# A routed expert layer: the first rows are fetched by an index of their own, without their records

## The chip, the cores and the metric

The kernel runs on one core of one Trainium2 chip. The metric is the device time of one execution in microseconds, from the program's start to its end. "The trace" is what the hardware profiler recorded of one such execution.

## The reference

Two blocks follow one another on 2048 rows of 512 numbers, all in float32. The first is a convolution layer (H3), the second a mixture of eight experts of which each row takes exactly one:

```
h  = x + q_layer(layernorm(x), k, v)          # short convolution, product, long convolution, gate
xf = layernorm(h)                             # 2048 x 512
logits = xf @ w_gate                          # 2048 x 8
topk_idx = argsort(-logits)[:, :1]
gates = softmax(topk_val)                     # over one value
for e in range(8):
    w   = (gates * (topk_idx == e)).sum(-1, keepdims=True)
    out = out + w * (silu(xf @ w1[e]) @ w2[e])   # w1[e]: 512 x 1792, w2[e]: 1792 x 512
result = h + out
```

Only the second block, its beginning above all, is touched by the change.

## The kernel before

**Stage 1.** The convolution layer is run in an order that a planner sets (`plan.run`, line 598); it writes the rows of h to a DRAM buffer, h_dram. The change leaves that order alone. What stage 1 leaves to the second block is h, the routing logits in `lacc`, and for each row a record `rec` of four numbers: mean, reciprocal standard deviation, gate weight and a helper for it. In before, a row of h_dram is 516 wide: 512 numbers of h and the four of the record behind them, so whoever fetches a row has its record too.

**Routing** (lines 601 to 727). All rows lie on 128 partitions with 16 rows each. VectorE finds the largest logit (`mx`, `eq`, `cand`, `oh`), a scan and three small products on TensorE count the rows of each expert (`pn`) and number them within it (`pr`). The experts are ordered by their number of rows: `key`, then `gt` and `sr` (rank of each expert), `perm_i` (which expert stands at which rank). Each row gets a place, `c_i` = its rank's place times 4096 and its number; split into a tile `col_i` and a position in the tile `lo_f`. To turn the map round (from places to rows), line 679 marks the tile of each row (`ohhi`, 24 tiles), lines 685 to 687 mark the position in 16 steps (`ohlo`, one instruction and one product for each of the 16 rows of a partition), and the products add up to `ptab`: the row at each place. From it come `idxg` (indices for fetching, line 694) and `idxs` and `half_i` (for storing). `keep_warm` puts products on TensorE whose result nobody reads.

**The start of the experts.** GpSimd fetches the first expert's rows by `idxg` (line 707) into two tiles, `first0` and `first1`; SyncE reads the first expert's number from `perm_i` and starts the loads of its first two weight pieces (line 715). A flag `wide_i` chooses between branches for row counts of different sizes; with these inputs the experts are given 240, 304, 280, 264, 256, 248, 240 and 240 rows in that order, in tiles of at most 128 rows.

**The experts** (`experts`, lines 730 to 943). Each expert has 14 steps, seven for w1 ("up") and seven for w2 ("down"), each with a weight piece of 128 x 1024 float32. All products are made of three products of parts: weights and rows are split into a high and a low part. A step's weights are loaded by SyncE (`raw`, eight steps ahead), split four steps ahead by ScalarE (`whi`) and VectorE (`wlo`). Up makes two blocks of 128 columns with 12 products each (line 821); ScalarE takes Silu (`s`, three buffers), VectorE the high part (`hh`) and GpSimd the low part (`hl`, line 826). Down (lines 842 and 845) reads hh and hl. While one expert runs, the next one's rows are fetched (`gather`, line 759: one tile each in the last steps of up), normalised on VectorE with the row's mean and reciprocal deviation (`norm`, line 772), transposed on TensorE in the fourth, fifth and sixth step of down (`turn_x`, line 781) and split again (lines 782, 783). Finished rows are scaled and added to h on VectorE (`o`, line 856) and scattered to the output by an indirect DMA that GpSimd issues (line 857). The last expert's last tile is done in two halves at the very end (`store_by_halves`).

**Order.** Each engine takes its instructions in the order in which the program issues them; an indirect DMA stands in GpSimd's queue between its other instructions. At the end all engines pass a common block (shown at line 1119), in which GpSimd and SyncE drain their queues.

## Time and profile before

| what | value |
|---|---|
| median of three timed runs | 544.11 us (543.62 to 544.54) |
| the profiled execution | 544.39 us |
| its span, first to last instruction | 542.5 us |
| mean granted TensorE clock, as a share of 2.4 GHz | 0.991 |
| TensorE busy, share of the span | 519.1 us, 96% |
| VectorE, ScalarE, GpSimd busy | 405.6, 265.1 and 260.7 us |
| memory read, written | 95.96 MB, 8.47 MB |

The profiled execution's time is 1.9 us longer than its span; this lies outside the recorded instructions. Busy shares are averages over stages with different limits, so the stretches and the order in time below are of more use than the shares. In the rows, PE is TensorE's product, PEld its weight load, DVE VectorE, ACT ScalarE, POOL GpSimd and SP SyncE; a letter q behind an engine's name marks what its sequencer does. "L686" is line 686 of the kernel.

### The profile page before, as it was taken

What the parts mean: (1) busy time and instruction counts of PE and PEld (TensorE: products, weight loads), DVE (VectorE), ACT (ScalarE), POOL (GpSimd) and SP (SyncE); (2) the same over time, 40 slices, a digit from 0 to 9 for tenths busy, and PEclk for the clock granted to TensorE, in tenths of its full rate; (3) what the DMA queues carried; (4) which work ended last, traced back from release to release, by engine and by line L of the source; (5) the groups of instructions that cost most, each with busy time, mean ns of one, the idle gap of its engine ahead of it and who ended that gap; (6) DMA issues with size and microseconds to landing.
All of it is one profiled execution on the core that took longest, in us unless ns stands there. A gap on an engine that the chain in (4) does not pass through costs nothing. (4 is left out here: it accounts for less than half of the span.)

```text
span 542.5 us, 12152 instructions
## 1 busy us (share of the span) xinstructions
PE 519.1 (96%) x4812; PEld 451.9 (83%) x4812; DVE 405.6 (75%) x558; ACT 265.1 (49%) x410; POOL 260.7 (48%) x297
## 2 busy tenths in 40 slices
PE   9999989999998699999999999999999999999994
PEld 9867767767656469789999999999988988988973
DVE  3779899898997968859855784974884784785851
ACT  2697887544320346545435445545543644554520
POOL 0555659865641136618503921840760760851832
PEclk9999999999999989999999999999999999999998
DMA  8918786659661278674654665674676566576401
GB/s 285 380 55 261 236 276 195 179 153 287 187 170 43 60 263 320 218 256 166 199 182 140 204 199 166 189 259 141 206 219 233 180 210 231 194 219 205 155 2 41
DMA packets 42468, 105.26 MB, mean 194 GB/s; under 512 B 6480, under 2 KB 14800, under 8 KB 42018
## 3 DMA queue, kind: packets, MB, share of 16 engines
q1 hardware_dynamic: 39602, 95.89, 54.9%
q0 software_dynamic: 2800, 8.51, 4.9%
q8 instruction: 40, 0.66, 0.5%
q14 instruction: 26, 0.21, 0.1%
HBM read 95.96 MB, written 8.47 MB: 193 GB/s over the span
## 5 line engine op out<-in xcount | busy, mean ns | idle before, releaser
L826 POOL TENSOR_TENSOR hl<-s,hh 128x240 fp32r<-128x240 f32 (+5 forms) x112 | 114.4, 1035 | 162.2 <-DVE hh L825 161.7
L807 DVE TENSOR_TENSOR wlo<-raw,whi 128x1024 fp32r<-128x1024 f32 x112 | 160.5, 1443 | 38.8 <-ACT whi L806 35.2
L806 ACT ACTIVATE whi<-raw 128x1024 fp32r<-128x1024 f32 x112 | 114.6, 1051 | 3.5 <-DMA raw<-in_w_dram 3.5
L824 ACT ACTIVATE s<-acc 128x240 f32<-128x240 f32 (+5 forms) x112 | 43.1, 387 | 98.1 <-PE acc L821 63.4
L825 DVE CAST hh<-s 128x240 fp32r<-128x240 f32 (+5 forms) x112 | 55.0, 501 | 30.1 <-ACT s L824 29.9
L821 PE MATMUL acc<-xh,whi 128*128 128x240 f32 (+5 forms) x448 | 73.0, 285 | 0.1
L821 PE MATMUL acc<-xh,wlo 128*128 128x240 f32 (+5 forms) x448 | 72.0, 283 | 0.0
L821 PE MATMUL acc<-xl,whi 128*128 128x240 f32 (+5 forms) x448 | 71.9, 283 | 0.0
L821 PEld LDWEIGHTS acc<-xh,whi 128*128 128x128 f32 x448 | 61.7, 189 | 0.8 <-ACT xh L782 0.3
L821 PEld LDWEIGHTS acc<-xl,whi 128*128 128x128 f32 x448 | 61.6, 189 | 0.0
L821 PEld LDWEIGHTS acc<-xh,wlo 128*128 128x128 f32 x448 | 61.4, 189 | 0.0
L842 PE MATMUL acc<-whi,hh 128*128 128x512 f32 (+2 forms) x136 | 54.3, 399 | 0.0
L842 PE MATMUL acc<-whi,hl 128*128 128x512 f32 (+2 forms) x136 | 53.6, 394 | 0.0
L842 PE MATMUL acc<-wlo,hh 128*128 128x512 f32 (+2 forms) x136 | 53.5, 394 | 0.0
L265 POOL TENSOR_TENSOR acc<-acc,ac 128x512 f32<-128x512 f32 x26 | 33.1, 1280 | 37.1 <-ACT acc L253 19.2
L845 PE MATMUL acc<-hh,whi 128*128 128x304 f32 (+2 forms) x168 | 49.8, 296 | 0.0
L845 PE MATMUL acc<-hl,whi 128*128 128x304 f32 (+2 forms) x168 | 49.2, 293 | 0.0
L845 PE MATMUL acc<-hh,wlo 128*128 128x304 f32 (+2 forms) x168 | 49.1, 292 | 0.0
L296 ACT ACTIVATE st<-pa 128x512 f32<-128x512 f32 x64 | 37.3, 595 | 20.6 <-PE pa L293 20.3
L293 PEld LDWEIGHTS pa<-kv,tw 128*128 128x128 f32 x256 | 30.2, 191 | 12.2 <-ACT st L296 8.7
L293 PE MATMUL pa<-kv,tw 128*128 128x128 f32 x256 | 33.5, 282 | 2.2 <-ACT st L296 2.2
L782 ACT ACTIVATE xh<-pt 128x512 fp32r<-128x512 f32 (+5 forms) x18 | 9.6, 535 | 53.1 <-PE pt L781 53.1
(171 smaller groups left out, 878.2 us busy)
## 6 DMA issues: line engine op xcount, KB each, us to landing
raw<-in_w_dram SPq DMA_DIRECT2D x112, 512.0 KB
tv<-in_tab_v_dram SPq DMA_DIRECT2D x12, 512.0 KB
h<-in_q_dram SPq DMA_DIRECT2D x16, 256.0 KB
kt<-in_kt_dram SPq DMA_DIRECT2D x3, 1216.0 KB
v<-in_v_dram SPq DMA_DIRECT2D x12, 256.0 KB
kern<-in_ssm_dram SPq DMA_DIRECT2D x12, 256.0 KB
h<-in_x_dram SPq DMA_DIRECT2D x12, 256.0 KB
h_dram<-h SPq DMA_DIRECT2D x12, 256.0 KB
```

What stands on the lines that cost most here:

```text
L265: nc.gpsimd.tensor_add(T[a, c, u], T[a, c, u], T[b, c, u])
L293: nc.tensor.matmul(p[:, :, j], tw[:, u * UJ + j, r, :], src[:, j, :], start=True, stop=True)
L296: nc.scalar.activation(T["s" + kind, c][:, r * NU + u], T["pa", kind, c, u, r], AF.Copy)
L782: nc.scalar.activation(xh[:, at, r0:r0 + m], pt[:, :, :m], AF.Copy)
L806: nc.scalar.activation(whi, raw, AF.Copy)
L807: nc.vector.tensor_sub(wlo, raw, whi.bitcast(F32))
L821: nc.tensor.matmul(pu, a[:, k, fs], b[:, k, :], start=i == 0, stop=i == 3 * ND - 1)
L824: nc.scalar.activation(s, pu, AF.Silu)
L825: nc.vector.tensor_copy(hh[:, f, :], s)
L826: nc.gpsimd.tensor_sub(hl[:, f, :], s, hh[:, f, :].bitcast(F32))
L842: nc.tensor.matmul(pd[:ds_.stop - ds_.start], b[:, f, ds_], a[:, f % 2, :], start=f == 0 and i == 0, stop=f == last - 1 and i == 2)
L845: nc.tensor.matmul(pd, a[:, f % 2, ds_], b[:, f, :], start=f == 0 and i == 0, stop=f == 2 * NCH - 1 and i == 2)
```

## The change

The first expert's rows get a table of their own. Instead of ranking all experts first, VectorE takes the smallest key (`least`), whose last bits are that expert's number, and only two tiles (`tile0`) are marked for it (`there0`, `m0`). The places no longer hold the rank: they are the expert's number times 4096, given by one more product into `pr`, and the row's number. The 16 one-hot instructions become two, on 16-bit integers with both operands as tensors, over nine and seven of the 16 rows. A product with `m0` gives `ptab0`, from which `idx0` fetches the rows. All 24 tiles (`m24`), the ranks, `eqm_p` and `perm_i` follow behind it, and `other_tables` later sorts the table into the order of the experts.

Rows and records have buffers of their own in DRAM: a row of h_dram is 512 wide, `rec_dram` holds the four numbers of each row. Mean and reciprocal deviation of the first expert's rows are not fetched: they are split into three bf16 parts, marked (`v0`) and selected by 16 products with the one-hot matrix (`pv0`, `mr0`). For all other experts each tile is fetched by two indirect DMAs, first the rows' ones, then the records'.

Further: up makes its two blocks side by side (all products with the first pair of parts, then the second, then the third); `wlo` of the first weight piece is made in two halves; the three last scatters stand behind the branches instead of within them, from three tiles of their own (`ends`); the warm-up products are placed differently.

On VectorE in the routing, behind the places `c_i`; ohhi and ohlo_f are the marks of tile and position, pt is the table in PSUM. Before:

```order
L674 TENSOR_REDUCE c_i<-r_2402 128x16
L675 TENSOR_SCALAR col_i<-c_i 128x16
L676 SCALAR_TENSOR_TENSOR lo_f<-col_i,c_i 128x16
L679 TENSOR_TENSOR ohhi<-tile_b,col_i 128x384
L686 TENSOR_SCALAR ohlo_f<-iota_b,lo_f 128x128 x16
L691 TENSOR_TENSOR over<-key,rungs 1x128
L693 TENSOR_REDUCE nover<-over 1x16
L694 TENSOR_SCALAR idxg<-pt 128x24
```

The same place after the change, up to the marks of all tiles; kt is a buffer of tables that also holds iota, tile and the first rows:

```order
L684 TENSOR_REDUCE c_i<-r_2420 128x16
L685 TENSOR_SCALAR col_i<-c_i 128x16
L686 TENSOR_SCALAR lo_i<-c_i 128x16
L692 TENSOR_TENSOR kt<-kt,col_i 128x32
L693 TENSOR_TENSOR m_2425<-kt,tok_b 128x32
L705 TENSOR_TENSOR ohlo_f<-kt,lo_i 128x128x9
L705 TENSOR_TENSOR ohlo_f<-kt,lo_i 128x128x7
L714 TENSOR_SCALAR idx_78<-pt 128x2
L715 RECIPROCAL rec<-rec 128x16
L716 TENSOR_TENSOR rec<-rec 128x16
L719 TENSOR_TENSOR over<-key,rungs 1x128
```

The index for the first rows stands ahead of a reciprocal and the flags, and is made from two marks instead of sixteen. On GpSimd in the first expert, from the middle of up to the second expert's first hl (hr are the rows of the next expert; two hl are one step). Before:

```order
L826 TENSOR_TENSOR hl<-s,hh 128x240 x8
L1119 ISA
L759 DMA hr_12846<-h_dram,idxg 128x516
L826 TENSOR_TENSOR hl<-s,hh 128x240 x2
L1119 ISA
L759 DMA hr_12888<-h_dram,idxg 128x516
L826 TENSOR_TENSOR hl<-s,hh 128x240 x2
L1119 ISA
L759 DMA hr_12930<-h_dram,idxg 48x516
L826 TENSOR_TENSOR hl<-s,hh 128x240 x2
L826 TENSOR_TENSOR hl<-s,hh 128x304 x3
```

After the change, from the third gather of rows on (what stands ahead of it is as before, with rows of 512):

```order
L823 DMA hr_13112<-h_dram,idxg 48x512
L895 TENSOR_TENSOR hl<-s,hh 128x240 x2
L1205 ISA
L823 DMA rec_13163<-rec_dram,idxg 128x4
L1205 ISA
L823 DMA rec_13179<-rec_dram,idxg 128x4
L1205 ISA
L823 DMA rec_13203<-rec_dram,idxg 48x4
L1205 ISA
L823 DMA rec_13245<-rec_dram,idxg 128x4
L1205 ISA
L823 DMA rec_13272<-rec_dram,idxg 112x4
L895 TENSOR_TENSOR hl<-s,hh 128x304 x3
```

Five fetches of records have come behind the first expert's last hl: three for the second expert's tiles, and two for the first expert's own, whose gate weights are needed when its rows are stored.

The diff, cut to what the text speaks of:

```diff
-    h_dram = dram.tile([S, RW], F32, name="h_dram")
+    h_dram = dram.tile([S, D], F32, name="h_dram")
+    rec_dram = dram.tile([S, 4], F32, name="rec_dram")
...
+    iota_b = place_h[:, :P * NJ].rearrange("p (m j) -> p m j", j=NJ)
+    tile_b = place_h[:, P * NJ:(P + 24) * NJ].rearrange("p (c j) -> p c j", j=NJ)
...
+    nc.gpsimd.tensor_scalar(base_b, const("e").unsqueeze(2).to_broadcast([P, E, NJ]), 32.0, None, op0=ALU.mult)
+    nc.gpsimd.tensor_copy(tile_b, const("tile").unsqueeze(2).to_broadcast([P, 24, NJ]))
+    nc.gpsimd.tensor_copy(iota_b, const("iota").unsqueeze(2).to_broadcast([P, P, NJ]))
...
-    keep_warm(5, 128)
+    pr = ps_t.tile([P, E, NJ], F32, name="pr", bufs=1)
+    nc.tensor.matmul(pr, one_b, base_b, start=True, stop=False)
+    keep_warm(8, 128)
...
+    rest = eq[:, 0:2]
+    both = rec[:, :, 0:2].rearrange("p j i -> p i j")
+    nc.gpsimd.tensor_copy(parts[:, 0], both)
+    nc.gpsimd.tensor_sub(rest, both, parts[:, 0])
...
-    nc.gpsimd.tensor_mul(rec[:, :, 2], rec[:, :, 2], rec[:, :, 3])
-    nc.sync.dma_start(h_rows[:, :, D:RW], rec)
...
+    least = small([1], "least", I32)
+    with nc.allow_low_precision(reason="whole numbers under 32768"):
+        nc.vector.tensor_reduce(least, key, axis=AX.X, op=ALU.min)
+    nc.vector.tensor_scalar(least, least, E - 1, None, op0=ALU.bitwise_and)
+    for t in range(2):
+        nc.gpsimd.tensor_scalar(tile0[:, t], least.to_broadcast([P, NJ]), 32.0, float(t), op0=ALU.mult, op1=ALU.add)
...
+    r2 = small([E, NJ], "r2")
+    nc.vector.tensor_tensor(r2, pr, oh, op=ALU.mult)
+    with nc.allow_low_precision(reason="whole numbers under 32768"):
+        nc.vector.tensor_reduce(c_i, by_j(r2), axis=AX.X, op=ALU.add)
+    nc.vector.tensor_scalar(col_i, c_i, 7, None, op0=ALU.logical_shift_right)
+    nc.vector.tensor_scalar(lo_i, c_i, P - 1, None, op0=ALU.bitwise_and)
+
+    def marks(name, tiles_b, n):
+        there = m = small([n, NJ], name, F16)
...
+        nc.vector.tensor_tensor(there, tiles_b, col_i.unsqueeze(1).to_broadcast([P, n, NJ]), op=ALU.is_equal)
+        nc.vector.tensor_tensor(m, there, tok_b.unsqueeze(1).to_broadcast([P, n, NJ]), op=ALU.mult)
+        return there, m
+
+    there0, m0 = marks("m0", tile0, 2)
...
+    for i in range(3):
+        for w in range(2):
+            nc.gpsimd.tensor_tensor(v0[:, i, w], there0, parts[:, i, w].unsqueeze(1).to_broadcast([P, 2, NJ]), op=ALU.mult)
+    ohlo = ohlo_f.bitcast(F16).rearrange("p (m j) -> p m j", j=NJ)
+    ptab0 = ps_t.tile([P, 2], F32, name="pt")
+    for js in (range(0, 9), range(9, NJ)):
+        at = slice(js[0], js[-1] + 1)
+        nc.vector.tensor_tensor(ohlo[:, :, at], iota_b[:, :, at],
+                                lo_i[:, at].unsqueeze(1).to_broadcast([P, P, len(js)]), op=ALU.is_equal)
+        for j in js:
+            nc.tensor.matmul(ptab0, ohlo[:, :, j], m0[:, :, j], start=j == 0, stop=j == NJ - 1)
+    pv0 = ps_t.tile([P, 12], F32, name="pt")
+    for j in range(NJ):
+        nc.tensor.matmul(pv0, ohlo_f.bitcast(BF16).rearrange("p (m j) -> p m j", j=NJ)[:, :, j],
+                         v0[:, :, :, :, j].rearrange("p i w t -> p (i w t)"), start=j == 0, stop=j == NJ - 1)
+    keep_warm(1, 512)
+    nc.vector.tensor_scalar(idx0, ptab0, -1.0, 0.0, op0=ALU.add, op1=ALU.max)
+    nc.vector.reciprocal(rec[:, :, 2], rec[:, :, 3])
+    nc.vector.tensor_mul(rec[:, :, 2], rec[:, :, 2], rec[:, :, 3])
...
+    m24 = marks("m24", tile_b, 24)[1]
+    mr0 = small([2, 2], "mr0")
+    nc.vector.tensor_reduce(mr0, pv0.rearrange("p (i w t) -> p t w i", i=3, w=2), axis=AX.X, op=ALU.add)
+    nc.vector.tensor_scalar(mr0, mr0, 128.0, None, op0=ALU.mult)
+    ptab = ps_t.tile([P, 24], F32, name="pt")
+    for j in range(NJ):
+        nc.tensor.matmul(ptab, ohlo[:, :, j], m24[:, :, j], start=j == 0, stop=j == NJ - 1)
+    keep_warm(3, 384)
...
-    ohhi = small([NJ, 24], "ohhi", F16)
-    nc.vector.tensor_tensor(ohhi, tile_b.unsqueeze(1).to_broadcast([P, NJ, 24]), bc(col_i, 24),
-                            op=ALU.is_equal)
-    vt = small([NJ, 24], "vt", F16)
-    nc.gpsimd.tensor_tensor(vt, ohhi, bc(tok_b, 24), op=ALU.mult)
-    ohlo = ohlo_f.bitcast(F16).rearrange("p (j m) -> p j m", j=NJ)
-    ptab = ps_t.tile([P, 24], F32, name="pt")
-    for j in range(NJ):
-        nc.vector.tensor_scalar(ohlo[:, j, :], iota_b, lo_f[:, j:j + 1], None, op0=ALU.is_equal)
-        nc.tensor.matmul(ptab, ohlo[:, j, :], vt[:, j], start=j == 0, stop=j == NJ - 1)
-    keep_warm(4, 432)
...
-        hr = first.tile([P, RW], F32, name=f"first{t}")
-        col = 3 * ORDER[0] + t
         nc.gpsimd.indirect_dma_start(
-            out=hr, out_offset=None, in_=h_dram[:, :],
-            in_offset=bass.IndirectOffsetOnAxis(ap=idxg[:, col:col + 1], axis=0))
-        rows0.append(hr)
-    place0 = nc.sync.value_load(perm_i[0:1, ORDER[0]:ORDER[0] + 1], min_val=0, max_val=E - 1)
+            out=rows0[t], out_offset=None, in_=h_dram[:, :],
+            in_offset=bass.IndirectOffsetOnAxis(ap=idx0[:, t:t + 1], axis=0))
+    place0 = nc.sync.value_load(least[0:1], min_val=0, max_val=E - 1)
     raw0 = []
     for ch in range(2):
         raw = first.tile([P, 1024], F32, name=f"raw{ch}")
         nc.sync.dma_start(raw, w1[bass.ds(place0, 1), ch].rearrange("o p f -> (o p) f"))
         raw0.append(raw)
-
+    nc.sync.dma_start(rec_dram.rearrange("(p j) d -> p j d", j=NJ), rec)
...
+    def other_tables():
+        nc.vector.tensor_tensor(sel, eqm_p.unsqueeze(2).to_broadcast([P, E, 3, E]),
+                                tabs_e.rearrange("p e t -> p t e").unsqueeze(1).to_broadcast([P, E, 3, E]), op=ALU.mult)
+        nc.vector.tensor_reduce(tabs, sel.rearrange("p i t e -> p (i t) e"), axis=AX.X, op=ALU.add)
+        nc.vector.tensor_scalar(idxg, tabs, -1.0, 0.0, op0=ALU.add, op1=ALU.max)
...
+        def gather(n, i):
+            ts = tiles(n)
+            if i >= 2 * len(ts):
+                return
+            kind, src, width = ("hr", h_dram, D) if i < len(ts) else ("rec", rec_dram, 4)
+            t, r0, m, col = ts[i % len(ts)]
+            into = X[kind, n, t] = xp.tile([P, width], F32, name=f"{kind}{t}")
+            nc.gpsimd.indirect_dma_start(
+                out=into[:m, :], out_offset=None, in_=src[:, :],
+                in_offset=bass.IndirectOffsetOnAxis(ap=idxg[:m, col:col + 1], axis=0))
...
+            pus = [ps_u.tile([P, cap], F32, name="acc") for _ in fs]
+            for i, (a, b) in enumerate(((whi, xh), (wlo, xh), (whi, xl))):
+                for f, pu in zip(fs, pus):
+                    at = slice((f % 2) * P, (f % 2) * P + P)
+                    for k in range(ND):
+                        nc.tensor.matmul(pu, a[:, k, at], b[:, k, :], start=i == k == 0, stop=i == 2 and k == ND - 1)
+            for f, pu in zip(fs, pus):
+                s = xp.tile([P, cap], F32, name="s", bufs=3)
+                nc.scalar.activation(s, pu, AF.Silu)
+                nc.vector.tensor_copy(hh[:, f, :], s)
+                nc.gpsimd.tensor_sub(hl[:, f, :], s, hh[:, f, :].bitcast(F32))
...
+        def send(n, t, m, y, rows, at, o=None):
+            late = o is not None
+            o = (o if late else xp.tile([P, D], F32, name="o", bufs=3))[:m]
+            nc.vector.scalar_tensor_tensor(o, y, X["rec", n, t][:m, 2:3], rows, op0=ALU.mult, op1=ALU.add)
+            if not late:
+                scatter(out, at, o, S)
...
-        gather(0)
+                send(n, t, m, pd[:m], X["part"][:m, cols], None, ends[half + 1])
+
+        firsts, last = tiles(0)[:-1], tiles(0)[-1]
         for s in range(len(raw0)):
             load_w(s)
-        split(0)
-        norm(0, *tiles(0)[0])
+            split_hi(s)
+        norm(0, *firsts[0])
+        split_lo(0, 0, 512)
         for s in range(len(raw0), AHEAD):
             load_w(s, s < 6)
-        for a in tiles(0)[1:-1]:
+        for a in firsts[1:]:
             norm(0, *a)
         for half in range(2):
-            norm(0, *tiles(0)[-1], half)
-        for a in tiles(0)[:-1]:
+            norm(0, *last, half)
+        split_lo(0, 512, 1024)
+        for a in firsts:
             turn_x(0, *a)
+        warm = ps_u.tile([P, P], F32, name="acc")
+        for _ in range(3):
+            nc.tensor.matmul(warm, const("one"), cs[:, :P], start=True, stop=True)
         for half in range(2):
-            turn_x(0, *tiles(0)[-1], half)
-        for s in range(1, LEAD):
+            turn_x(0, *last, half)
+        split_lo(1)
+        other_tables()
+        for s in range(2, LEAD):
...
+                if r < 2 and n + 1 < E:
+                    gather(n + 1, r + 4)
+                if n == 0 and 3 <= r < 3 + len(tiles(0)):
+                    gather(0, r - 3 + len(tiles(0)))
                 if 3 <= r < 3 + len(nx):
                     turn_x(n + 1, *nx[r - 3])
...
+    scatter(out, idxs[:, end - 1:end], ends[0], S)
+    for i in range(2):
+        scatter(halves, half_i[:, i:i + 1], ends[i + 1], 2 * S)
```

## Rows read from the trace of the kernel before

**Rows 1.** The table of stretches: start and end in us, length, then busy us and number of instructions of PE, PEld, DVE, ACT and POOL, the granted TensorE clock (share of full), the DMA engines' busy share, GB/s. The first row is the routing, the next four are pieces of it, then the experts, then the tail.

```profile
182.30:198.56 16.26, 11.82 (x56) 7.47 (x56) 12.38 (x54) 5.65 (x11) 6.62 (x14) 0.79 0.44 117
184.45:187.87 3.42, 1.67 (x13) 1.42 (x12) 3.13 (x14) 2.19 (x5) 0.51 (x2) 1.00 0.22 8
187.87:191.28 3.41, 2.25 (x15) 1.54 (x15) 3.41 (x18) 0.00 (x0) 0.83 (x1) 0.50 0.27 29
191.28:194.70 3.42, 3.42 (x7) 1.83 (x8) 0.88 (x7) 1.25 (x2) 2.16 (x2) 0.50 0.86 310
194.70:198.56 3.86, 2.84 (x12) 1.26 (x11) 3.02 (x10) 1.00 (x3) 2.44 (x6) 1.00 0.64 186
198.56:534.80 336.24, 336.24 (x2384) 315.18 (x2384) 239.58 (x280) 161.39 (x253) 156.54 (x148) 1.00 0.59 195
534.80:542.50 7.70, 0.00 (x0) 0.00 (x0) 0.48 (x1) 0.00 (x0) 1.45 (x2) 0.80 0.18 58
```

**Rows 2.** The timeline of VectorE: a two-source f32 instruction from the end of stage 1, then the routing. Columns: start in us, duration in us, engine, line, operation, out and in with their shapes, number of instructions in the row (its duration is that of all of them), and in brackets idle time before it and what ended that.

```profile
172.35 0.69 DVE L372 TENSOR_TENSOR st<-st 128x512 f32<-128x512 f32 x1
...
183.48 0.26 DVE L627 RECIPROCAL rec<-rec 128x16 f32<-128x16 f32 x1
...
185.33 0.17 DVE L652 SCALAR_TENSOR_TENSOR key<-pn,cs 128x8 f32<-128x8 f32 x1
185.53 0.23 DVE L657 TENSOR_TENSOR gt<-key 128x64 f32<-128x64 f32 x1
...
186.19 0.27 DVE L668 SCALAR_TENSOR_TENSOR r<-sr,pt 128x128 f32<-128x128 f32 x1
186.49 0.29 DVE L670 TENSOR_TENSOR r<-r,oh 128x128 f32<-128x128 f32 x1
186.70 0.20 DVE L672 TENSOR_REDUCE perm_i<-eqe 1x8 int32<-1x64 f32 x1
186.83 0.35 DVE L674 TENSOR_REDUCE c_i<-r 128x16 int32<-128x128 f32 x1
...
187.52 0.55 DVE L679 TENSOR_TENSOR ohhi<-tile_b,col_i 128x384 f16<-128x384 bf16 x1
187.99 3.32 DVE L686 TENSOR_SCALAR ohlo_f<-iota_b,lo_f 128x128 f16<-128x128 f16 x16
...
191.73 0.16 DVE L694 TENSOR_SCALAR idxg<-pt 128x24 int32<-128x24 f32 x1
```

**Rows 3.** The timeline from the index to the first product of the first expert, all engines, columns as in rows 2; between them two weight loads of warm-up products (PEld), and below the summary of line 707's DMAs (time from issue to landing).

```profile
192.20 1.20 POOL L707 DMA_INDIRECT first<-h_dram,idxg  x1 [3.22 <-DVE wide_i L697]
192.99 0.34 PEld L607 LDWEIGHTS warm<-cs 128*128 128x128 f32 x1 [0.38 <-issue]
193.71 0.34 PEld L607 LDWEIGHTS warm<-cs 128*128 128x128 f32 x1 [0.38 <-issue]
194.67 1.22 DVE L807 TENSOR_TENSOR wlo<-raw,whi 128x1024 fp32r<-128x1024 f32 x1 [2.47 <-ACT whi L806]
195.82 0.55 DVE L772 TENSOR_SCALAR xr<-first 128x512 f32<-128x512 f32 x1
196.31 0.09 DVE L797 MEMSET raw<- 128x1 f32 x4
197.24 0.74 DVE L772 TENSOR_SCALAR xr<-first 112x256 f32<-112x256 f32 x2 [0.84 <-DMA first<-h_dram,idxg]
198.56 0.71 PE L821 MATMUL acc<-xh,whi 128*128 128x240 f32 x3
...
DMA to landing us min/median/max: 3.5/3.5/3.5
```

**Rows 4.** The timeline of the first expert's hl chain on GpSimd and of the handover to the second expert, columns as in rows 2; below the summary of the 17 gathers of line 759.

```profile
206.60 3.89 POOL L826 TENSOR_TENSOR hl<-s,hh 128x240 fp32r<-128x240 f32 x4 [9.19 <-DVE hh L825]
...
214.42 2.35 POOL L826 TENSOR_TENSOR hl<-s,hh 128x240 fp32r<-128x240 f32 x2 [0.23 <-DVE hh L825]
...
223.21 0.90 POOL L759 DMA_INDIRECT hr<-h_dram,idxg  x1 [0.16 <-issue]
224.12 1.39 POOL L826 TENSOR_TENSOR hl<-s,hh 128x240 fp32r<-128x240 f32 x2
226.53 0.54 DVE L772 TENSOR_SCALAR xr<-hr 128x512 f32<-128x512 f32 x1
227.35 0.60 PE L781 MATMUL pt<-cs,xr 128*128 128x128 f32 x4
...
DMA to landing us min/median/max: 3.6/4.0/4.6
```

**Rows 5.** The tail: two rows of the timeline, and two of the view of the last line (number of instructions, duration in ns min/median/max, first and last start in us).

```profile
534.84 0.48 DVE L856 SCALAR_TENSOR_TENSOR o<-acc,hr,part 112x256 f32<-112x256 f32 x1 [0.92 <-PE acc L886]
535.61 0.95 POOL L857 DMA_INDIRECT out_dram<-o,half_i  x1 [0.30 <-POOLq L948]
...
L1119 POOLq DRAIN  x3: 46/102/3311, 538.3 to 542.2; - x3
L1119 SPq DRAIN  x3: 7/7/13, 540.4 to 541.9; - x3
```

**Rows 6.** The handover from the third expert to the fourth in the timeline, columns as in rows 2.

```profile
314.00 1.54 POOL L826 TENSOR_TENSOR hl<-s,hh 128x280 fp32r<-128x280 f32 x2
316.56 0.54 DVE L772 TENSOR_SCALAR xr<-hr 128x512 f32<-128x512 f32 x1
320.80 0.60 PE L781 MATMUL pt<-cs,xr 128*128 128x128 f32 x4
```

More of the change, by code (lines that the diff above doesn't have):

```diff
@@ L12 @@
 I32 = mybir.dt.int32
+I16 = mybir.dt.int16
 AF = mybir.ActivationFunctionType
@@ new lines @@
+    over = small([2, E, E], "over", parts=1)
+    nc.vector.tensor_tensor(over, key[0:1].unsqueeze(1).unsqueeze(1).to_broadcast([1, 2, E, E]), rungs, op=ALU.is_gt)
+    nover = small([2, E], "nover", parts=1)
+    nc.vector.tensor_reduce(nover, over, axis=AX.X, op=ALU.add)
+    nc.vector.tensor_tensor(nover, nover, const("e")[0:1].unsqueeze(1).to_broadcast([1, 2, E]), op=ALU.is_gt)
+    with nc.allow_low_precision(reason="0 or 1"):
+        nc.vector.tensor_reduce(wide_i, nover, axis=AX.X, op=ALU.max)
@@ L691 @@
-    nc.vector.tensor_tensor(over, key[0:1].unsqueeze(1).unsqueeze(1).to_broadcast([1, 2, E, E]), rungs, op=ALU.is_gt)
-    nover = small([2, E], "nover", parts=1)
-    nc.vector.tensor_reduce(nover, over, axis=AX.X, op=ALU.add)
-    nc.vector.tensor_scalar(idxg, ptab, -1.0, 0.0, op0=ALU.add, op1=ALU.max)
-    nc.vector.tensor_tensor(nover, nover, const("e")[0:1].unsqueeze(1).to_broadcast([1, 2, E]), op=ALU.is_gt)
-    with nc.allow_low_precision(reason="0 or 1"):
-        nc.vector.tensor_reduce(wide_i, nover, axis=AX.X, op=ALU.max)
```

195 lines of the change are left out of this document (93 added, 102 removed).

## Prediction

> **What bounds the kernel now.** I read the busy times of the page first, then a table of stretches, then the timeline of the routing, of the first expert and of the tail. The reader is to see in the table of stretches [rows 1] that TensorE is busy for the whole of every stretch from 198.56 to 534.80 us: from the first product of the first expert on, its time is the time. Outside that, two pieces count: the 16.26 us from 182.30 to 198.56, in which the routing decides, the first rows are fetched and TensorE mostly does warm-up products, and the 7.70 us after 534.80. So the change can act in three ways: the first product comes earlier or later, TensorE comes to wait somewhere after it, or the tail changes.
>
> In the routing, VectorE is busy nearly all the time up to the end of idxg [rows 2]: key at 185.33, c_i at 186.83, then 16 one-hot instructions in 3.32 us, then idxg, which ends at 191.73 + 0.16 = 191.89. GpSimd issues the two row gathers from 192.20, the second lands 3.5 us after its issue, the halves of its tile are normalised from 197.24 and the first product of the expert starts at 198.56: 6.67 us after idxg's end [rows 3].
>
> In the first expert there is a second chain beside TensorE [rows 4]. The GpSimd instructions hl run from 206.60, nearly without a gap at the end, with the three gathers of the next expert's rows between them; the last pair's end is 224.12 + 1.39 = 225.51. VectorE normalises the next expert's first tile from 226.53 to 227.07, and TensorE comes to that tile's transposes at 227.35. TensorE doesn't wait there, but only by 0.28 us.
>
> In the tail [rows 5] the last o is ready at 535.32, the last scatter's issue ends at 536.56, and then GpSimd starts its DRAIN only at 538.32 and ends it at 538.32 + 3.31 = 541.63. SyncE's own DRAIN is at 540.4.
>
> **The change part by part.** The profiled execution took 544.39 us with a span of 542.5; the sum is made against 544.39. The three timed runs have a median of 544.11, 0.28 lower, and I take that off at the end.
>
> *Index of the first rows.* Before the one-hot instructions the chain loses a reciprocal (0.26 long; I count 0.24), the steps gt, sr and eqm (185.53 to 186.19: 0.66), the first of the two r (186.19 to 186.49: 0.30) and perm_i (186.70 to 186.83: 0.13), 1.33 in all, and gains two steps for the smallest key (0.45, an estimate from key's 0.17 and perm_i's 0.20 with their gaps); the two marks of 32 elements cost about 0.4 where ohhi took 0.47. That is 0.95 less [rows 2]. The 16 one-hot instructions become two of 16-bit numbers with two sources, 2,048 elements a partition. No row of before has such an instruction. Upper bound: two-source f32 rows, 0.69 us at 512 and 1.22 us at 1,024 elements [rows 2, 3], about 1.02 ns an element, so 2 x 0.15 + 2.1 = 2.4 us. Lower bound: the one-source 16-bit rows, 3.32/16 = 0.21 for 128 elements against 0.16 for 24 [rows 2], about 0.4 ns an element with the fixed part, so 1.15 us. I take 1.2, since the 16-bit row is nearer: 2.1 less than 3.32. Against that, all seven products of the second group now follow the second instruction, where before only one followed the last: 15 products took 2.25 us at the half clock [rows 1], 0.15 each, so 0.9 more. idx0 ends at 191.89 - 0.95 - 2.1 + 0.9 = 189.7 (189.3 with TensorE at full clock, 191.2 with the upper bound and some slack).
>
> The Trainium skill, "VectorE: DVE Perf Modes", section "The perf-mode tier table", gives two-source instructions on 16-bit numbers two elements a cycle and f32 ones a single one. By that page the pair would be near my lower bound; no run here shows it yet.
>
> *From the index to the first product.* The fetch is as long as before. But VectorE now does after idx0 what it did before it: six short instructions (reciprocal, product, over, three for wide_i) of 0.16 to 0.27 us each [rows 2], together about 1.3; marks over 384 elements twice (0.55 each as ohhi), the sums of the records (0.4), gt, sr, eqm, eqe, perm_i (1.1): about 4.1 us. The first tile's normalisation comes at idx0 + 4.1 (193.8; before 195.82), then half a wlo, then the four memsets that release the weight loads, at idx0 + 5.35 = 195.05 against 196.31: 1.2 earlier. The fetch lands at idx0 + 5.35 too; the second tile is normalised at idx0 + 5.6; from there 1.32 as before and 0.6 for three new warm-up products and the longer queue. The first product then starts at 189.7 + 7.5 = 197.2, 1.4 earlier. Both records and weights are there by then.
>
> TensorE's granted clock was 0.50, the 1.2 GHz level, from 187.87 to 194.70, after a stretch in which its small products filled only 1.67 of 3.42 us; it was back at full after 3.42 us without a gap [rows 1]. The new queue has 32 more small products and other warm-ups, so this can fall out differently: at half clock throughout, the queue alone would hold the first product until about 200.3 (189.7, then two tables of 16 products at 0.15, four wide ones of two passes each at about 0.7, as the passes follow each other from 192.99 to 193.71 [rows 3], and 0.3 for what is left before the transposes).
>
> *Handover to the second expert.* This is the step that decides. The rows of the next expert no longer bring their mean and rstd: those come by a gather of their own, and the issue of it stands on GpSimd behind hl number 14, the last. In before the last of the rows' gathers is issued at 223.21, ahead of the last pair. That chain is bound by GpSimd and by weights that come 1.2 earlier: the last pair ends at 225.51 - 1.2 = 224.3. Then 0.14 to the issue, the landing (3.6 to 4.6 us in 17 gathers of L759 [rows 4]; 3.5 in the first two [rows 3]; I take 3.3 for rows of 16 bytes, an estimate below the shortest), 0.08, and 0.54 for the normalisation: 228.4. TensorE arrives at 227.35 - 1.4 = 225.95 and waits 2.4 us; from there it is 228.4 - 227.35 = 1.0 later than before. The gain of the start is gone, and 1.0 more. With a landing of 4.0 and nothing gained at the start it is 2.9; with GpSimd's chain 0.7 shorter still it is 0.3.
>
> *Later experts.* They have cover: for the third, hl ends at 315.54, normalisation starts at 316.56, and the transposes come at 320.80 [rows 6]. A landing of 3.3 and the records' issue after 315.54 give 319.5, still ahead. The other 19 small DMAs at about 1.0 us each lie on GpSimd, which is busy for under half of the time from 198.56 on [rows 1]: nothing.
>
> *Tail.* The three last scatters leave the If block. GpSimd is then past its branch long before the end, so the 1.76 us from 536.56 to 538.32 can't fall there. If the DRAIN only waits for the scatter to land, nothing is gained; if it has a fixed length, SyncE's end at 540.5 takes over and 1.2 is gained. I take 0.6.
>
> The Trainium skill, "Runtime: NRT & Kernel Launch", section "Instruction fetch mechanics", says that a taken branch to code that isn't loaded stalls the engine. The trace agrees with such a gap: branch at 535.44, next instruction at 538.32. By that page 1.76 would go from GpSimd's end; SyncE's rows allow 1.2 at most.
>
> *Sum:* 544.39 + 1.0 - 0.6 = 544.8, less 0.28: **544.5 us**.
>
> **The rivals.** *Slower:* the two one-hot instructions run at the f32 rate (2.4 us). The index then comes 1.2 later than assumed, the weight loads and with them the hl chain are not earlier than before, and TensorE waits at the handover until 225.51 + 0.14 + 3.3 + 0.62 = 229.6: 2.2 later than before. With the tail 544.39 + 2.2 - 0.6 - 0.28 = 545.7; with a landing of 4.0, 546.4. For it: no row shows the 16-bit rate. Against: the 16-bit row. It decides as soon as TensorE is late by more than the tail gives plus 1.1. The half clock lasting through the new queue belongs to the same side: first product at 200.3, TensorE at the handover at 229.1, 1.8 late, 545.2.
>
> *Faster:* the records are there before TensorE wants them, since the hl chain is 2.4 us shorter or records land much faster than rows. Then the start's 1.4 stays: 544.39 - 1.4 - 0.6 - 0.28 = 542.1, and 541.5 with the tail in full. For it: the chain has waits for s and for VectorE that earlier weights could shorten. Against: from 214.42 on GpSimd has no gap of over 0.4 [rows 4].
>
> *The change doesn't do what it says:* the index is earlier, but VectorE's moved work holds the first product at 198.5. Then only the handover and the tail count: 545.0, within the forecast's own range.
>
> **How the numbers follow.** The forecast case, its last form with it, 0.39, own range 543.6 to 545.6; faster 0.33; slower by the one-hot rate 0.21, by the clock 0.07. A difference of under 0.2% (1.09 us) can't be told from none here: faster is under 543.0, slower over 545.2. Of the forecast case about 0.03 falls under 543.0, a few hundredths over 545.2, and of the clock's case half falls within: faster 0.36, same 0.37, slower 0.27. The range 541.9 to 546.2 reaches into both other cases and leaves about 0.1 out on either side.
>
> **What would show it.** idx0 near 189.7 and the pair of one-hot instructions at 1.2 us; the first product at 197.2; TensorE idle for about 2.4 us before the transposes of the second expert's first tile, ended by VectorE's normalisation, which itself waits for the records' gather; no such wait in later experts; GpSimd's DRAIN starting right behind the last scatter. It is wrong if TensorE has no gap at the handover, if the one-hot pair takes over 2 us, or if a new wait appears in a later expert.

## The result and the profile after

| | before | after |
|---|---|---|
| median, lowest to highest (7 runs each) | 544.11 us, 543.59 to 544.65 | 548.53 us, 546.38 to 550.47 |
| profiled execution, its span | 544.39, 542.5 us | 549.19, 547.3 us |
| ratio after/before, 95% interval | | 1.0076, 1.0051 to 1.0101 |

The change makes the kernel slower by 4.4 us, and its runs spread over 4.1 us where those of before spread over 1.1. The forecast of 544.5 us was wrong, and the range, up to 546.2, doesn't hold the time.

The table of stretches of the changed kernel, with the columns of [rows 1], cut at the routing's first product (181.69), the first expert's first product, the wait at the handover, the second expert's first product and the last product:

```profile
181.69:198.20 16.51, 15.44 (x107) 12.64 (x108) 12.44 (x49) 6.48 (x12) 7.13 (x19) 0.79 0.36 115
198.20:226.68 28.48, 28.48 (x210) 26.42 (x210) 23.55 (x31) 17.73 (x28) 22.36 (x24) 1.00 0.83 298
226.68:229.38 2.70, 0.39 (x2) 0.00 (x0) 0.60 (x2) 0.00 (x0) 2.09 (x3) 1.00 0.33 111
229.38:233.24 3.86, 3.86 (x12) 3.11 (x13) 3.86 (x5) 1.54 (x2) 2.87 (x3) 0.56 0.36 134
233.24:242.20 8.96, 8.96 (x44) 6.81 (x44) 6.77 (x8) 3.77 (x5) 0.00 (x0) 1.00 0.77 249
242.20:538.75 296.55, 296.42 (x2121) 279.79 (x2119) 203.32 (x239) 137.66 (x217) 156.95 (x145) 1.00 0.56 182
538.75:547.27 8.52, 0.00 (x0) 0.00 (x0) 0.48 (x1) 0.00 (x0) 1.49 (x2) 0.80 0.16 51
```

Where [rows 1] had one row without a gap, there are now two odd pieces: 2.70 us in which TensorE works for 0.39, and 3.86 us at a mean granted clock of 0.56. TensorE's waits in the changed kernel name the first piece (engine and line, what it waited for, us in total, times, longest):

```profile
PE pt L845 <- DVE xr L836: 2.3, 1, 2.3
```

The timeline of the handover, to be laid beside [rows 4]:

```profile
223.40 2.46 POOL L895 TENSOR_TENSOR hl<-s,hh 128x240 fp32r<-128x240 f32 x2
...
226.01 0.98 POOL L823 DMA_INDIRECT rec<-rec_dram,idxg  x1 [0.16 <-issue]
...
228.78 0.55 DVE L836 TENSOR_SCALAR xr<-hr,rec 128x512 f32<-128x512 f32 x1 [4.16 <-DMA rec<-rec_dram,idxg]
...
229.38 0.74 PE L845 MATMUL pt<-cs,xr 128*128 128x128 f32 x4 [2.31 <-DVE xr L836]
...
231.21 0.63 PE L911 MATMUL acc<-whi,hh 128*112 128x512 f32 x1
...
233.53 0.39 PE L911 MATMUL acc<-whi,hh 128*112 128x512 f32 x1
```

The record's fetch follows the last hl, VectorE waits for it and TensorE for VectorE, as forecast. Then comes what was not forecast: the same product takes 0.63 us at 231.21 and 0.39 at 233.53. The granted clock was at its 1.2 GHz level for 3.42 us right behind the wait (columns as in [rows 1]):

```profile
229.82:233.24 3.42, 3.42 (x11) 2.67 (x9) 3.42 (x5) 1.54 (x2) 2.73 (x2) 0.50 0.41 152
233.24:236.00 2.76, 2.76 (x15) 2.19 (x15) 2.65 (x4) 1.15 (x2) 0.00 (x0) 1.00 0.86 256
```

Half of 3.42 is 1.71 us lost, an estimate that takes all of TensorE's work there, where it was busy throughout, at half speed. From the first expert's first product to the second's it is 43.97 us (198.20 to 242.17), before 39.96 (198.56 to 238.52): 4.01 more, and 2.31 + 1.71 = 4.02. The account of the profiled executions: start 0.36 earlier, first expert 4.01 longer, the others 0.30 longer (296.30 from 242.17 to the last product's start, 538.47; before 296.00), from there to the end 8.80 instead of 7.95: in all 4.80, the difference of the two times. The tail's end in the view of the last line, to be laid beside [rows 5]:

```profile
L1205 POOLq DRAIN  x3: 46/108/7101, 539.3 to 547.0; - x3
L1205 SPq DRAIN  x3: 7/7/13, 544.8 to 546.7; - x3
```

In the routing VectorE's rows answer to [rows 2]: the pair of one-hot instructions took 1.65 us, and the index for the first rows starts at 189.70. From there to the first product three rows matter: the warm-up products of 384 columns, the normalisation of the first tile and its transposes.

```profile
185.59 0.17 DVE L666 SCALAR_TENSOR_TENSOR key<-pn,cs 128x8 f32<-128x8 f32 x1 [1.19 <-PE pn L660]
...
187.35 1.65 DVE L705 TENSOR_TENSOR ohlo_f<-kt,lo_i 128x1152 f16<-128x1152 int16 x2
...
189.70 0.16 DVE L714 TENSOR_SCALAR idx<-pt 128x2 int32<-128x2 f32 x1 [0.70 <-PE pt L708]
...
192.89 3.56 PE L623 MATMUL warm<-cs 128*128 128x384 f32 x6
...
194.82 0.55 DVE L836 TENSOR_SCALAR xr<-kt,mr 128x512 f32<-128x512 f32 x1 [1.15 <-issue]
...
196.29 0.60 PE L845 MATMUL pt<-cs,xr 128*128 128x128 f32 x4
```

### The profile page after: what moved, and what is told of

Its sections match the earlier page's. It is cut to its first block, busy times and chain, and to the rows that moved or that the text cites. A ratio compares the mean times of both kernels' runs of the same rounds, so it can differ in the third digit from the quotient of the medians.

```text
span 547.3 us, 12304 instructions
## 1 busy us (share of the span) xinstructions
PE 523.8 (96%) x4863; PEld 456.9 (83%) x4863; DVE 404.1 (74%) x556; ACT 265.2 (48%) x410; POOL 291.5 (53%) x329
## 4 chain that ended last, share of the span: by engine, by line
PE 77%; DMA 8%; DVE 5%; issue 4%; ACT 3%; POOL 1%; POOLq 0%; DVEq 0%
PE acc L890 26%; PE acc L911 13%; PE acc L914 12%; PE pa L295 8%; PE pb L331 7%; DMA kt<-h_dram,idx 6%; PE pa L367 5%; PE pa L449 2%; PE pm L279 2%; DMA kt<-in_kt_dram 1%; PE pt L845 1%; DVE xa L344 1%; DVE zs L352 1%; PE pt L934 1%; DVE bst L381 1%
## 5 line engine op out<-in xcount | busy, mean ns | idle before, releaser
L895 POOL TENSOR_TENSOR hl<-s,hh 128x240 fp32r<-128x240 f32 (+5 forms) x112 | 118.4, 1070 | 131.0 <-DVE hh L894 130.3
L872 DVE TENSOR_TENSOR wlo<-raw,whi 128x1024 fp32r<-128x1024 f32 (+1 forms) x113 | 161.9, 1443 | 35.3 <-ACT whi L867 35.1
L894 DVE CAST hh<-s 128x240 fp32r<-128x240 f32 (+5 forms) x112 | 52.7, 481 | 30.7 <-ACT s L893 30.5
```

The lines of the kernel that those rows point to most:

```text
L872: nc.vector.tensor_sub(wlo[:, a:b], RAW[s][:, a:b], whi[:, a:b].bitcast(F32))
L894: nc.vector.tensor_copy(hh[:, f, :], s)
L895: nc.gpsimd.tensor_sub(hl[:, f, :], s, hh[:, f, :].bitcast(F32))
```

## The experiments

The numbering leaves out 8. Each time stands beside that of the kernel before on the same chip. "First expert" is the time from its first product to the second expert's first product, from the timeline of the run's profile (before: 39.96 us, changed kernel: 43.97). The kernel before differs by up to 0.8 us between these measurements, so where two runs with different times of it are compared below, each is counted from its own; the changed kernel stands 4.42 us above it (548.53, 544.11).

| run | median, kernel before beside it | ratio, 95% interval | first expert | TensorE's waits there |
|---|---|---|---|---|
| e1 | 546.31, 544.89 | 1.0029, 1.0014 to 1.0043 | 40.75 | 0.6 |
| e2 | 548.59, 544.89 | 1.0075, 1.0057 to 1.0092 | 42.85 | 0.6 and 2.3 filled |
| e3 | 550.63, 544.89 | 1.0109, 1.0090 to 1.0128 | 45.00 | 3.2 |
| e4 | 548.49, 544.89 | 1.0073, 1.0049 to 1.0098 | 41.87 | 1.8 |
| e5 | 549.51, 544.35 | 1.0085, 1.0069 to 1.0101 | 46.12 | 4.9 |
| e6 | 544.04, 544.35 | 0.9992, 0.9983 to 1.0000 | 39.94 | none |
| e7 | 546.06, 544.35 | 1.0032, 1.0020 to 1.0045 | 39.87 | none |
| e9 | 546.62, 544.35 | 1.0037, 1.0024 to 1.0051 | 43.17 | 2.2 |
| e10 | 544.40, 544.50 | 0.9994, 0.9974 to 1.0014 | 39.92 | none |
| e11 | 543.84, 544.50 | 0.9984, 0.9964 to 1.0004 | 39.92 | none |
| e12 | 543.62, 544.26 | 0.9978, 0.9963 to 0.9994 | 39.91 | none |
| e13 | 544.46, 544.26 | 1.0003, 0.9991 to 1.0015 | 40.00 | none |

**e1, records between the rows.**

```diff
-            kind, src, width = ("hr", h_dram, D) if i < len(ts) else ("rec", rec_dram, 4)
-            t, r0, m, col = ts[i % len(ts)]
+            if n:
+                kind, src, width = (("hr", h_dram, D), ("rec", rec_dram, 4))[i % 2]
+                t, r0, m, col = ts[i // 2]
...
```

> The changed kernel with one edit: the fetches for the next expert go rows 0, record 0, rows 1, record 1, and so on, instead of all rows first. Theory: TensorE's 2.3 us wait at the handover to the second expert exists because the record's fetch is issued behind the last hl, and the half clock that follows it (229.8 to 233.2) costs another 1.7 us. Then the wait at the transposes of that tile goes, the granted clock stays at full from the first product to the end, and the time falls by 4.0, to about 544.5 (changed kernel: 548.5), with little spread between runs. Rival, the records' landing or VectorE's order decides: a wait of 1 us or more stays there and the time is 546.5 or above. Rival, the half clock comes from something else: the wait goes, the clock still falls, about 546.3.

1.4 us above the kernel before, where the changed kernel is 4.4 above: 3.0 less, not 4.0. The second rival's 546.3 is met by number only, since in this profile the clock doesn't fall at the handover. The first tile's wait and the half clock are gone (43.97 to 40.75), but the wait moved on to later tiles, whose rows and records are now fetched later. TensorE's waits of that run (us in total, times, longest):

```profile
PE pt L849 <- DVE xr L840: 1.6, 3, 0.7
```

**e2, the wait filled.**

```diff
+                if n == 0 and r == 3:
+                    for _ in range(3):
+                        nc.tensor.matmul(ps_u.tile([P, 432], F32, name="acc"), const("one"), cs[:, :432],
+                                         start=True, stop=True)
```

> The changed kernel with three products of 432 columns that nobody reads ahead of the second expert's first transposes, about 2.2 us of TensorE's time, inside its wait of 2.3 us. Theory, the clock falls because TensorE is idle there: the transposes start at the same place, but the clock stays at full behind them; 1.7 less than the changed kernel, about 546.8, and less spread between runs. Rival, the half clock there has another cause: time and clock as in the changed kernel, about 548.5.

In the profile the clock stays full behind the handover and the first expert is 42.85 us: 1.13 less than in the changed kernel, with 2.34 of filling and a wait of 0.56 in place of 2.31 + 1.71. The forecast gain of 1.7 doesn't show in the medians (3.7 us above the kernel before, against 4.4), with spreads of 1.9 and 4.1 us. So the clock's share is told by the profiles alone: of the four runs that waited there without filling and for nothing else, the two with a half-clock stretch behind it (the changed kernel, e3) have a first expert of 39.96, the wait and 1.7 to 1.8 more; e1 and e4, without such a stretch, have 39.96, the wait and 0.1 to 0.2 more.

**e3, the last scatters inside the branch; e4, with e1's edit too.**

```diff
+            elif o.shape[-1] == D:
+                scatter(out, idxs[:m, end - 1:end], o, S)
+            else:
+                half = y_half[0]
+                scatter(halves, half_i[:m, half:half + 1], o, 2 * S)
...
-    scatter(out, idxs[:, end - 1:end], ends[0], S)
-    for i in range(2):
-        scatter(halves, half_i[:, i:i + 1], ends[i + 1], 2 * S)
```

> The changed kernel with the last three scatters issued inside the branch, each behind its o, as in the kernel before. Theory, leaving the branch early made the tail longer (from the last o's end to the end of the span 8.0 us against 7.15 before): the tail is 7.2 and the time 0.8 lower, about 547.7, though the spread of the changed kernel can hide that. Rival, the tail's length differs from run to run for other reasons: 7.7 to 8.1. By the prediction as it was put the tail would be longer by 0.6 or more than in the changed kernel: 8.6.

> Both edits, records between the rows and the last scatters inside the branch. By the theories above: no wait at the handover, full clock, tail 7.2: about 543.7, 0.4 below the kernel before, which is what the start has gained (first product at 198.20 against 198.56). Rival, the tail isn't set by the place of the scatters: as the run with records between alone, about 544.5.

The theory on the tail fell, and its rival too: with the scatters inside, the kernel is slower in both pairs, by 2.2 us in e4 against e1 and by 1.3 in e3 against the changed kernel. From the last product's start to the end of the span it is 9.64 and 9.69 us in e3 and e4, against 8.80 in the changed kernel and 8.14 in e1. The view of the last line in e3 shows why (columns as in [rows 5]):

```profile
L1210 POOLq DRAIN  x3: 46/102/4863, 542.9 to 548.3; - x3
```

DRAIN lasts 4.86 us there, 4.86 in e4 too, against 3.31 in [rows 5]. What has grown is the number of indirect DMAs that GpSimd issued in the run. By the rows of GpSimd's groups it is 18 + 17 + 2 + 2 = 39 before, and 17 + 17 + 2 + 2 + 1 = 39 and 19 fetches of records now:

```profile
L823 POOL DMA_INDIRECT rec<-rec_dram,idxg x19 | 20.7, 1090 | 4.2 <-issue 4.2
```

**e7, the kernel before with 19 fetches that nobody reads; e6, the kernel before with the scatters behind the branches.**

```diff
+                    nc.gpsimd.indirect_dma_start(
+                        out=xp.tile([P, 4], F32, name="unread")[:m, :], out_offset=None, in_=rec_dram[:, :],
+                        in_offset=bass.IndirectOffsetOnAxis(ap=idxg[:m, col:col + 1], axis=0))
```

> The kernel before with 19 more small fetches by GpSimd of records that nobody reads, at places where GpSimd is idle (the first steps of down, in the first expert the fourth and fifth too). Theory: DRAIN 4.8 to 5.0 us instead of 3.31, the time 1.5 higher than the kernel before, and nothing else changes. Rival, the 4.86 us of the runs with the scatters inside come from the last tiles or from where the last fetches stand: DRAIN 3.3, time as before.

> The kernel before with the tail of the change alone: the last three scatters behind the branches, from three tiles of their own. Theory: GpSimd's DRAIN takes a time for each indirect DMA that it has issued in the whole run (39 of them: 3.31 us in the kernel before; 58: 4.86 us in the two runs with the scatters inside), and the change of place takes away only what lay between the last scatter's issue and the DRAIN (1.76 us). So: from the last scatter's issue to the DRAIN's end 3.4 to 3.6 us instead of 5.07, and the time 1.5 lower than the kernel before. Rival, a fixed wait for the last scatter's landing: 5 us stay, no gain.

e7, then e6, each by the view of its last line:

```profile
L1127 POOLq DRAIN  x3: 46/102/4865, 537.6 to 543.0; - x3
```

```profile
L1130 POOLq DRAIN  x3: 46/108/5155, 534.9 to 540.6; - x3
L1130 SPq DRAIN  x3: 7/7/13, 538.9 to 540.3; - x3
```

e7 came out as expected: 58 DMAs, DRAIN 4.87 us, 1.7 us slower with TensorE's stretches unchanged. So 19 more indirect DMAs lengthen it by 1.56 us, about 0.08 each if all cost the same (only two counts were run), and it doesn't matter whether they are read. e6 gained less than expected. The DRAIN no longer begins late, but it ends 3.92 us behind the last scatter's issue (536.13 to 540.05), not 3.5, and the median is 0.3 lower, not 1.5; the profiled execution (542.83) is the shortest of its eleven.

With the scatters behind the branches the DRAIN's end follows SyncE's own drain instead: 1.06 to 1.11 us behind it in e6 and e9 to e13 (39 and 41 DMAs), 1.65 to 1.82 in the changed kernel, e1, e2 and e5 (58). There 17 to 19 more DMAs cost 0.5 to 0.8 us, not 1.56. Why it is so, no run shows.

**e5, records before the rows.** The records of the next expert are fetched in the first three steps of up.

```diff
-                if 3 <= r and n + 1 < E:
-                    gather(n + 1, r - 3)
+                if n + 1 < E:
+                    gather(n + 1, r - 3)
```

(Indices below zero are the records.)

> The changed kernel with the next expert's records fetched in the first three steps of up, ahead of its rows, which keep their places. Theory (the handover's wait and the half clock behind it are one cost, made by the records' late issue; with records between the rows the wait only went on to later tiles, 1.6 us in three places): no wait of TensorE for a normalisation from the first product to the end, the granted clock at full there, 336 us from the first to the last product as in the kernel before (340.3 in the changed kernel). Time about 544.5 where the kernel before has 544.5. Rival, three more fetches of about 1 us in the GpSimd chain of the first expert make the rows late instead: a wait of about 1 us at the second or third tile, 545.5.

A miss, and worse than its rival. The fetches now stand between the hl, and TensorE waits for s, whose three buffers hl empties (ScalarE's s waited for hl 11.5 us in the first expert, in the changed kernel 6.5). TensorE's waits, the last line from a later expert:

```profile
PE pt L851 <- DVE xr L842: 2.1, 1, 2.1
PE acc L896 <- ACT s L899: 1.6, 2, 1.0
PE acc L917 <- ACT s L899: 1.2, 1, 1.2
PE acc L920 <- ACT s L899: 0.8, 2, 0.5
```

At none of the three places tried (behind hl, between the rows, ahead of them) did the first expert take the records without a wait.

**e9, e10, records behind the rows again.** Rows of 516 for all but the first expert; the new routing and the tail are kept, and 41 indirect DMAs are left. In e9 the records are stored ahead of the weight loads, in e10 after ten of them.

```diff
-            kind, src, width = ("hr", h_dram, D) if i < len(ts) else ("rec", rec_dram, 4)
+            if n and i >= len(ts):
+                return
+            kind, src, width = ("hr", h_dram, RW) if n else ("rec", rec_dram, 4)
...
+            if s == 1:
+                nc.sync.dma_start(h_rows[:, :, D:RW], rec)
```

> The changed kernel with records behind the rows again for all experts but the first (rows of 516; the first expert's gate weights still come from the buffer of records): 41 indirect DMAs instead of 58, and no fetch of records for the second to eighth experts. By the theories: no wait at the handovers, 336 us from the first to the last product, the first product 0.4 us earlier than in the kernel before or up to 1.3 as the clock falls out, DRAIN 3.5 us right behind the last scatter. Time 544.5 - 0.4 - 1.5 = 542.6 where the kernel before has 544.5. Rival, the separate records aren't the cause of the changed kernel's loss: 546 or more.

> The kernel of the run rows-with-records with one edit: the records are stored behind the rows not ahead of the weight loads but after ten of them (there the store waited for the rows' fetch until 194.6 and the third weight piece came at 202.1 instead of 199.6). Theory: the first expert's up is again 18.9 us long and no wait for weights is left; at the handover TensorE waits by what the start has gained over 0.3 us, since the normalisation of the next tile stands behind hl, Silu and the splits, which start no earlier. So from the first product to the second expert's first product 40.0 to 41.0 us (before 39.9, changed kernel 44.0), and the time between 0.8 below and 0.3 above the kernel before. Rival, the rows of 516 or the late store cost elsewhere: 1 us or more above it.

e9 missed by a fault of its own, though its time is what the rival forecast (546 or more). The store goes out only at 194.64, behind the rows' fetch, and then 2048 pieces of 16 bytes travel with the weights, whose loads are issued no later than in the changed kernel (195.90 against 196.02). Timeline of e9:

```profile
194.64 0.54 SPq L765 DMA_DIRECT2D h_dram<-rec  x1
...
202.10 1.06 ACT L875 ACTIVATE whi<-raw 128x1024 fp32r<-128x1024 f32 x1 [4.75 <-DMA raw<-in_w_dram]
```

e10 moves that store alone, and is the run that decides: with the records back in the rows the 4.4 us are gone (ratio 0.9994), the first expert is 39.92 us, and TensorE doesn't wait at any handover. This is TensorE's only wait from 196 us to the last product, at the start of the first expert:

```profile
PE acc L897 <- ACT xh L853: 0.3, 1, 0.3
```

So the separate fetches of records cost the 4.4 us: in the profile of the changed kernel 4.0 at the first handover, the rest in the later experts and the tail. And the new routing and the new tail together bring nothing that can be measured.

**e11, as e10, tiles normalised a step earlier.**

```diff
-            if 1 <= r - NCH < 1 + len(nx):
-                norm(n + 1, *nx[r - NCH - 1])
+            if 0 <= r - NCH < len(nx):
+                norm(n + 1, *nx[r - NCH])
```

> As e10, and the next expert's tiles are normalised one step earlier on VectorE. Theory, the start's gain can only come through when the handover's chain is shortened too: no wait at the handover, 39.9 us from first product to first product, and all of the start's gain in the time: 1.3 below the kernel before in executions with a single stretch of half clock in the routing, 0 in those with two, and 0.2 to 1.0 more from the tail: a median of about 1 below. Rival, the start's gain is lost elsewhere (weights): as e10.

0.66 us below the kernel before, with an interval that includes no change. In its profile the time from the routing's first product to the expert's is 15.44 us (182.50 to 197.94) with the clock half for 3.4 us; in e10's it is 16.73 (182.43 to 199.16) with the clock half for 6.8.

**e12, e13, warm-up products.** e12 has 11 instead of 8 behind the numbering, e13 one of 384 columns instead of three ahead of the transposes, both on e11.

```diff
     nc.tensor.matmul(pr, one_b, incl, start=False, stop=True)
-    keep_warm(8, 128)
+    keep_warm(11, 128)
```

> As e11, with 11 instead of 8 warm-up products behind the numbering, which fills TensorE's gap of 0.6 us ahead of the products with the one-hot matrix. In the runs so far with the new routing the time from the first product of the routing (line 636 here) to the first expert's first product was 15.1 to 15.4 us where the granted clock was half in one stretch of 3.4 us, and 16.5 to 16.9 where it was half for two. Theory, the gap counts in the clock's fall: one stretch at most, 15.4 us or less, median 0.5 below e11 (543.3). Rival, the many small products there make the clock fall whatever stands ahead of them: as e11, 543.8.

> As e11, with one instead of three warm-up products of 384 columns ahead of the first transposes. Theory, at half clock these products (0.64 us a pass, two passes each) hold the transposes back, in the changed kernel until 196.29 with the rows normalised at 195.37: 0.3 to 0.9 less from the routing's first product to the expert's in executions with two stretches of half clock, nothing in the others; median 543.5. Rival, without them the clock stays half for longer, into the expert's first products: 544.5 or more.

e12 is 0.22% below the kernel before, 0.06 to 0.37; it can't be told from e11 (0.16% below). But the reason isn't shown to be the one given. Its profiled execution, the slowest of its twelve, has 6.8 us at half clock and takes 16.80 us there; the four fastest, 542.05 to 542.37, lie 1.1 us under the rest and may be those with 3.4, but no profile shows it. e13 gains nothing; in its profile the clock is half for 10.2 us.

## Why the prediction was wrong

- **What failed.** The sum of 544.8 stood 4.4 us below the profiled execution (549.19): 2.65 of it up to the second expert's first product, 1.45 in the tail, 0.30 in the later experts.
- **Index, right in mechanism, in this execution 0.8 late.** 189.70 forecast for its end, 189.86 measured; but the routing began 0.64 earlier here (181.69 against 182.33). From there it is 8.17 us, where 7.37 was forecast and 9.56 is before. In nine other profiles with the new routing it is 7.05 to 7.19; 8.17 here and 8.13 in e13 go with a stretch of half clock at the routing's start (182.04 to 185.45 here). The one-hot pair took 1.65 us, between the bounds of 1.15 and 2.4, not at the lower one, which comes out of its two rows at 1.24 (0.46 ns an element, not 0.4). The Trainium skill, "VectorE: DVE Perf Modes", section "The perf-mode tier table", gives such an instruction on 16-bit numbers (bf16 there) two elements a cycle, twice the rate of f32. The trace shows a gain over the 2.4 us worked out from the f32 rows of [rows 2, 3], but not a doubling.
- **First product, wrong by 1.0.** 197.2 forecast, 198.20 measured. Counted from the routing's first product the start gained nothing: 16.51 us against 16.23, where 14.9 was forecast. Two terms failed. The first tile's normalisation came 4.96 us behind the index instead of 4.1, in all eleven profiles with the new routing: VectorE stood idle for 1.15 us before it, and why isn't shown. The other is the clock. I gave a chance of 0.07 to "the half clock lasting through the new queue" and summed without it; here the tile was normalised at 195.37, but the transposes had to wait until 196.29 behind six warm-up passes, which took 3.56 us at partly half clock (2.96 in e4, 4.19 in e1). In the eleven profiles the time is 15.1 to 15.4 us where the clock was half for 3.4 us in all (e4, e5, e9, e11) and 16.5 to 17.0 where it was half for 6.8 us or more; with the old routing (before, e6, e7) it was 16.2 to 16.6. What brings one kind or the other, no run shows.
- **Handover, right in mechanism, wrong in price.** The term that failed is "from there it is 228.4 - 227.35 = 1.0 later than before": it took the wait as the whole price. The transposes came 2.0 later (229.38 against 227.35), and the clock at half from there on cost about 1.7 more, so TensorE came out of the first expert 3.65 us later than before (242.17 against 238.52). That the wait was 2.31 us where 2.4 was forecast is luck: TensorE came at 227.07 instead of 225.95, and the tile was ready at 229.33 instead of 228.4. Of the tile's chain two parts were off. The last pair of hl began 0.72 earlier than before (223.40 against 224.12), but took 2.46 us instead of 1.39 and so ended at 225.86 instead of 224.3; single hl of the first expert take 0.7 to 0.9 or 1.7 to 1.8 us in these profiles, and which comes when isn't explained by any run. The record was there 2.77 us after its issue began, where 3.3 was estimated; in e2 and e3, with the same order, it took 4.69 and 4.77, so the wait isn't the same in each execution.
- **Later experts, right.** No wait of TensorE for a record there, as forecast; 0.30 us more in all, whose cause isn't shown. (Up makes its two blocks side by side in the very first step only, not in all as the text on the change has it.)
- **Tail, gain not there.** 0.6 gained was forecast, 0.85 was lost in the profiled execution. The cover named was right: the 1.76 us between the last scatter's issue and the DRAIN are gone. The Trainium skill, "Runtime: NRT & Kernel Launch", section "Instruction fetch mechanics", says that a taken branch to code that isn't loaded stalls the engine. The trace agrees so far: a gap of 1.6 to 1.9 us stands ahead of the DRAIN in all four profiles in which the last scatters stand inside the branch (before, e3, e4, e7), and in none of the others. The step that failed is "nothing" for the 19 new DMAs: I took them to be free because GpSimd has time, and they are paid for in the DRAIN. The 0.85 itself is no firm number. From the last product's start to the end it is 8.80 us in the changed kernel, but 8.14, 8.06 and 7.75 in e1, e2 and e5 with the same tail, and 7.95 before; SyncE's drain came 6.30 us behind that product in the changed kernel and 4.9 to 5.9 in all other profiles. Without the move outside, the tail would be longer still (9.64 and 9.69 in e3, e4).
- **The rivals.** The slower rival had the right side and the wrong mechanism: its condition, the one-hot pair at 2.4 us, didn't come true (1.65), and e10 with the same routing is as fast as before. Its second form, the half clock, came in part: first product at 198.20, not 200.3. The third, with the first product held at 198.5, was near in time, but TensorE's queue held it and not VectorE's moved work. The faster rival's condition, records there in time, came true in e10, and even then the start gave nothing.

## What to carry to other kernels

A wait on TensorE in the middle of dense work is to be priced as the wait and, where the granted clock falls behind it, half of that stretch besides: here 2.3 us became 4.0. A small indirect DMA isn't free on an idle GpSimd: it lengthens the chain of whatever stands behind it there, and 19 of them lengthened the DRAIN at the end by 1.56 us (e7). And before an earlier start is counted as a gain, look for the first handover: with 0.28 us to spare, as in [rows 4], the chain beside TensorE has to be shortened by as much as the start gains beyond that.

## What the hardware showed that was not expected

- GpSimd's DRAIN at the end of the run, where the last scatters stand inside the branch: 3.31 us with 39 indirect DMAs, 4.86 to 4.87 with 58, to 0.01 us the same in three kernels (e3, e4, e7).
- A wait of 2.3 us by TensorE, in work that was dense before and after it, was followed by 3.42 us at half clock in the changed kernel and 3.2 us of waiting by 3.41 in e3, while 1.8 us of waiting in e4 and 2.1 in e5 were not.
- With 32 KB stored as pieces of 16 bytes just ahead of it, a 512 KB load came about 2.5 us later (e9: its split at 202.10, in the changed kernel 199.56). In the changed kernel the same numbers are stored in pieces of 256 bytes alone; in e10 the small pieces go out at 204.66, behind ten loads, and TensorE waits for no weights.
